# An mLSTM cell with a quick-GELU layer: order of the second chunk's loads, issuer of the first chunk's stores, order of the first gelus

## The chip, the cores and the metric

The kernel runs on one core of a Trainium2 chip. The metric is the device time of one execution in microseconds (us). A core has five engines that run side by side, each through its own list of instructions in order: PE (matmul), DVE (vector), ACT (scalar, with activation functions), POOL, and SP, which here only issues DMA transfers. They meet at semaphores.

## The reference

The first part is an mLSTM cell over 4 batches, 8 heads, 768 time steps and a head size of 40. The second is a feed-forward layer with the quick GELU.

```python
for t in range(S):
    m_new = np.maximum(f_gate[:, :, t] + m, i_gate[:, :, t])
    f_stab = np.exp(f_gate[:, :, t] + m - m_new)
    i_stab = np.exp(i_gate[:, :, t] - m_new)
    m = m_new
    C = f_stab * C + i_stab * einsum('bhd,bhe->bhde', v_t, k_t)
    n = f_stab * n + i_stab * k_t
    h_tilde = einsum('bhde,bhe->bhd', C, q_t)
    denom = np.maximum(np.abs(sum(n * q_t)), 1.0)
    y[:, :, t] = sigmoid(o_gate[:, :, t]) * h_tilde / denom
x = y.transpose(0, 2, 1, 3).reshape(B * S, H * D)      # 3072 x 320
h = x @ w_in                                            # 320 x 2048
out = (h * sigmoid(1.702 * h)) @ w_out                  # 2048 x 320
```

## The kernel before, in words

Time is cut into six chunks of 128 steps (`w` from 0 to 5). For each chunk the mLSTM is worked out as attention within the chunk plus a state carried from the chunks before; then the 512 rows of the chunk (4 batches of 128) go through the feed-forward layer. While the layer of chunk `w` runs on PE, the attention of chunk `w + 1` is put between its matmuls, in steps that `attention` lists.

No scheduler moves instructions. Each engine runs its instructions as the Python calls stand, so an instruction that waits holds back all behind it on its engine. Every DMA is given one of eight completion semaphores; before it is used again, its next user waits until the DMA that had it has landed. At most eight transfers are therefore under way from SP.

The parts that the change and the prediction touch:

- Loads. `load` brings a chunk's k, v or output gates (`eo`, 640 KB in one DMA; `eo` has one buffer). `load_blocks` brings k and q a second time in small blocks (`k_bl`, `q_bl`, 16 DMAs each) that DVE then transposes to `kT` and `qT` (L302). `spread` brings the rows of running maxima (`m_row`) to all partitions as `wt` (L317, 4 DMAs).
- Weights. 20 pieces come in by `fetch` (L166), 0 to 9 of `w_in` and 10 to 19 of `w_out`. They land in `big`, `bits` or `xs`, and `convert` turns each into its rounded form, with two instructions on ACT (L228, L229) and four on DVE (L232 to L237). Pieces 16 to 19 use rooms that pieces 10 to 12, or others, had before. The table `beside` says when pieces are converted and when later ones are fetched; pieces 16 and 17 hold rows of `w_out` that the third group of four of `down` (n = 2) reads.
- Chunk 0. The first two hidden blocks are multiplied before the main loop (`full_rows`, L714 and L737), and their gelus (L765) stand at the head of the loop. The others go through `up` (L458, L464, gelus L468). `down` (L561) then makes 16 blocks, four for each batch; the last of a batch copies the sum from PSUM (L565, DVE, into one of two `o_sb` buffers) and stores it (L566).
- Attention of chunk 1 beside those blocks: `columns`; `weights` (exponentials L335, POOL's mask L337; for batch 0 also the tanh of the gates, L340); `scores` (PE L348, DVE L350); `values` (PE L360 and L365, DVE L380 to L390); `seam` (transposes L399, and ACT's copy to `xT`, L400); `new_states` (L425) and `carry` (L433).
- Chunks 1 to 5. `up_fast` and `down_fast` take seven products of half-size blocks in place of eight. `up_fast` first makes sums of `xT` (L501 to L504), six products L513, then the remaining rows L541; sums on DVE are L521, gelus on ACT L525. In its first call `next_keys` stands between (sums of weights L489, the next chunk's `gates`, and transposes L302). The sums of `w_out` are L580.

SP's list in the stretch of interest is: pieces 10 to 15; the gates `eo` of chunk 1; 16 `k_bl`; 4 `wt`; pieces 16 and 17; 16 `q_bl`; v; pieces 18 and 19; k; the gates i and f of chunk 2; 16 `k_bl` and 16 `q_bl` of chunk 2; the four stores of chunk 0; then chunk 2's `m_row`.

Of the kernel before, what the change touches and what calls it, by code (L numbers as in the profile page):

```python
# [22 lines left out]
L = 128  # L23
# [11 lines left out]
def kernel(  # L35
# [12 lines left out]
    nc = tc.nc  # L48
    B, H, S, D = q.shape
# [44 lines left out]
    def load_gates(w):  # L94
        for dst, src in ((f_sb, f_gate), (i_sb, i_gate)):
            dst[w] = ld.tile([BH, L], FP, tag="fi", bufs=4, name="fi")
            nc.sync.dma_start(out=dst[w], in_=src[:, :, w * L:(w + 1) * L].rearrange("b h s -> (b h) s"))

    def load(w, what, bs=slice(0, B)):
        hs = slice(bs.start * H, bs.stop * H)  # L100
        for c in what:
            if c == "o" and w not in eo:
                eo[w] = ld.tile([L, BH, D], FP, tag="eo", bufs=1, name="eo")
            dst, src = {"k": (k_st, k), "q": (q_st, q), "v": (v_st, v), "o": (eo.get(w), o_gate)}[c]
            nc.sync.dma_start(out=dst[:, hs, 0:D],
                              in_=src[bs, :, w * L:(w + 1) * L, :].rearrange("b h s d -> s (b h) d"))

    def load_blocks(w, which=slice(0, 2)):
        both = (k_bl, k), (q_bl, q)
        for dst, src in both[which] if isinstance(which, slice) else both[which:which + 1]:  # L110
            for two in range(2):
                for d in range(0, D, 32):
                    n = min(32, D - d)
                    r = two * 64 + d
                    for g in range(L // 32):
                        t = w * L + g * 32
                        nc.sync.dma_start(
                            out=dst[r:r + 32, :, g, 0:n],
                            in_=src[:, two:H:2, t:t + 32, d:d + n].rearrange("b j s d -> s (b j) d"))
# [36 lines left out]
    def fetch(n):  # L156
        if 6 <= n < 10:
            bits[n] = gp.tile([128, 512, 2], U32, tag="g", name="bits")
        else:
            room = xs if n == 19 else big[:, n if n < 6 else (n - 10) % 6, :]  # L160
            bits[n] = room.bitcast(U32).rearrange("p (a two) -> p a two", two=2)
        for r, c, src in pieces[n][1]:
            dst = bits[n][r, c].rearrange("p a two -> p (a two)")
            if len(src.shape) == 3:
                dst = dst.rearrange("p (j m) -> p j m", j=src.shape[1])
            nc.sync.dma_start(out=dst, in_=src)  # L166
# [131 lines left out]
    def transposes(w, b):  # L298
        for bl, st, dst, name in ((k_bl, k_st, kT, "kT"), (q_bl, q_st, qT, "qT")):
            dst[w, b] = work.tile([128, NP, L], FP, tag=name, bufs=4, name=name)  # L300
            if w:
                V.transpose(out=dst[w, b].rearrange("p j t -> p (j t)"),  # L302
                            in_=bl[:, b * NP:(b + 1) * NP].rearrange("p j g c -> p (j g c)"))
                continue
            pt = ps_a.tile([128, NP, L], FP, tag="a", name="p_t")
            for p in range(NP):
                h = b * H + 2 * p
                T.transpose(pt[:, p, :], st[:, h:h + 2, :].rearrange("p a b -> p (a b)"), ident)
            if b == 0:
                keep_busy(1)  # L310
            A.copy(out=dst[w, b], in_=pt)

    def spread(w):

        for b in range(B):
            x = wt[w, b] = work.tile([L, NP, 2, L], FP, tag="wt", bufs=4, name="wt")
            nc.sync.dma_start(out=x.rearrange("s p i t -> s (p i) t"),  # L317
                              in_=m_row[w][b * H:(b + 1) * H, :].unsqueeze(0).to_broadcast([L, H, L]))
# [237 lines left out]
    def down(w, b, n):  # L556
        if n == 0:
            o_ps[w, b] = (ps_m if b < 2 else ps_x).tile([128, DM], FP, tag="mx"[b // 2], name="p_out")
        po = o_ps[w, b]
        for f in range(n * 4, n * 4 + 4):  # L560
            T.matmul(po, gs[w, f // 2][:, f % 2, b * L:(b + 1) * L], w_out_sb[:, f, :], start=(f == 0),  # L561
                     stop=(f == NF - 1))
        if n == NF // 4 - 1:
            o = op.tile([128, DM], FP, tag="o", name="o_sb")
            V.tensor_copy(out=o, in_=po)  # L565
            nc.sync.dma_start(out=out[b * S + w * L:b * S + (w + 1) * L, :], in_=o)  # L566

# [8 lines left out]
    def weight_sums(n):  # L578
        out_, in0, in1 = ((t1, w01, w00), (t2, w11, t1), (t4, w10, t2), (w01, w11, w01))[n]
        V.tensor_tensor(out=out_, in0=in0, in1=in1, op=OP.subtract)  # L580
# [153 lines left out]
    for j in range(2):  # L734
        for i in range(2):
# [2 lines left out]

    beside = {0: ((5,), range(10, 16)), 1: ((6, 7, 8), ()), 2: ((9, 10, 11), (16, 17)), 3: ((12, 13, 14), (18, 19)),
              4: ((15,), ()), 5: ((16,), ()), 10: ((17,), ()), 12: ((18,), ()), 14: ((19,), ())}

    def weights_in(n):
        done, ahead = beside.get(n, ((), ()))
        for p in done:
            convert(p)
        for p in ahead:
            fetch(p)
# [8 lines left out]
    for w in range(NW):  # L758
        more = w + 1 < NW
        for j in range(NF // 2):  # L760
            if w == 0 and j == 0:
                weights_in(0)
                for pair_ in range(2):
                    for i, g in enumerate(hidden_of(0, pair_)):
                        A.activation(out=g, in_=first[pair_][i], func=AF.Gelu_apprx_sigmoid)  # L765
            elif w == 0 and j % 2 == 0:
                weights_in(j // 2)
                up(j, j == 2)
            elif w and j % 4 == 0:
                up_fast(w, j, next_keys if more and j == 0 else None)  # L770
            if j == 0 and more:
                load(w + 1, "o")
            if w == 0 and j == 0:
                load_blocks(1, 0)
                spread(1)
            if w == 1 and j == 3:
                weight_sums(3)
            if more:
                if j == 4:
                    if w == 0:  # L780
                        load_blocks(1, 1)
                    load(w + 1, "v")
                    if w:
                        spread(w + 1)
                if j == (4 if w else 6):
                    load(w + 1, "k")
                if w and j == 3:
                    for b in range(2, 4):
                        transposes(w + 1, b)
            if w and j in (3, 7):  # L790
                hidden_sums(w, 0, (j // 4 * 2, j // 4 * 2 + 1), 1, 2)
                if j == 3:
                    hidden_sums(w, 0, (0, 1), 3, 4)
        side = attention(w + 1) if more else []
        if w == 0:

            blocks = [(lambda b=b, n=n: down(w, b, n)) for ns in ((0, 1), (2,), (3,)) for b in range(B) for n in ns]
            stops = (0, 1, 5, 7, 9, 11, 13, 15)
        else:
            blocks = down_fast(w, 0) + down_fast(w, 1)  # L800
            stops = (0, 1, 2, 4, 8, 10, 11, 12)
        for i, block in enumerate(blocks):
            if w == 0:
                weights_in(4 + i)
                if i == 0:
                    load_gates(2)
                if i == 2:
                    first_sums((0, 1))
                if i == 10:
                    load_blocks(2)  # L810
                for b in {2: (0, 1), 7: (2,), 9: (3,)}.get(i, ()):
                    transposes(1, b)
            elif w + 2 < NW and i == 0:
                load_gates(w + 2)
                load_blocks(w + 2)
            block()
            if i in stops and side:
                run(side.pop(0))
            if w == 1 and i == 1:
                weight_sums(2)  # L820
            if w:
                for at, c, *what in ((0, 0, (2, 3), 3), (1, 0, (2, 3), 4), (1, 1, range(4), 1),
                                     (5, 1, range(2), 2), (6, 1, range(2, 4), 2), (7, 1, range(4), 4)):
                    if i == at:
                        hidden_sums(w, c, *what)
                if i == 2 and not more:
                    hidden_sums(w, 1, range(4), 3)
            elif i in (12, 14):
                weight_sums(i // 2 - 6)
# [30 lines left out]
```

## Time and profile before

| | us |
|---|---|
| median of 9 runs | 490.92 |
| lowest and highest | 489.18, 495.72 |
| the profiled execution | 489.18 |
| its span | 487.5 |
| PE busy in it | 481.4 (99%) |
| DVE busy | 343.0 (70%) |
| ACT busy | 220.9 (45%) |
| POOL busy | 61.2 (13%) |

The profile is of one execution, the fastest of the nine. Its span runs from the first to the last instruction; 1.7 us of its time lie outside. A line of a timeline gives the start, the length, the engine, the line of the kernel, the operation, what it writes and reads, and in brackets the idle time before it and what ended that. Lines marked SPq are DMA issues, whose length is that of the issue; the transfer itself lands later. The chunks begin on PE's feed-forward products at about 24 us (chunk 0), 115 (chunk 1), 194, 270, 346 and 422.

### The profile page before, as it was taken

What the parts mean: (1) busy time and instruction counts of PE and PEld (TensorE: products, weight loads), DVE (VectorE), ACT (ScalarE), POOL (GpSimd) and SP (SyncE); (2) the same over time, 40 slices, a digit from 0 to 9 for tenths busy, and PEclk for the clock granted to TensorE, in tenths of its full rate; (3) what the DMA queues carried; (4) which work ended last, traced back from release to release, by engine and by line L of the source; (5) the groups of instructions that cost most, each with busy time, mean ns of one, the idle gap of its engine ahead of it and who ended that gap; (6) DMA issues with size and microseconds to landing.
All of it is one profiled execution on the core that took longest, in us unless ns stands there. A gap on an engine that the chain in (4) does not pass through costs nothing. (4 is left out here: it accounts for less than half of the span.)

```text
span 487.5 us, 10441 instructions
## 1 busy us (share of the span) xinstructions
PE 481.4 (99%) x4076; PEld 396.7 (81%) x4076; DVE 343.0 (70%) x855; ACT 220.9 (45%) x575; POOL 61.2 (13%) x103
## 2 busy tenths in 40 slices
PE   8999999999999999999999999999999999999997
PEld 5874456777678999787999877999977999977997
DVE  8789768887978965667776586686576786254831
ACT  6766767302458501476700465900364920255300
POOL 4030002231000340000332000232000120000000
PEclk9999999999999999999999999999999999999999
DMA  9999799563996200996100796300393000000000
GB/s 135 182 290 338 98 267 171 71 73 77 133 227 63 29 28 15 158 215 75 15 29 1 117 253 75 32 28 3 72 261 31 1 7 24 28 2 0 1 27 28
DMA packets 175953, 44.87 MB, mean 92 GB/s; under 512 B 164352, under 2 KB 169504, under 8 KB 175904
## 3 DMA queue, kind: packets, MB, share of 16 engines
q1 hardware_dynamic: 175904, 44.21, 48.4%
q8 instruction: 32, 0.52, 0.4%
q14 instruction: 17, 0.14, 0.1%
HBM read 40.17 MB, written 4.01 MB: 91 GB/s over the span
## 5 line engine op out<-in xcount | busy, mean ns | idle before, releaser
L610 PE MATMUL p_out<-w_out_sb,g 128*128 128x160 f32 x480 | 69.8, 301 | 0.0
L400 ACT COPY xT<-p_x 128x384 f32<-128x384 f32 x24 | 11.0, 480 | 128.0 <-PE p_x L399 128.0
L610 PEld LDWEIGHTS p_out<-w_out_sb,g 128*128 128x128 f32 x480 | 66.4, 190 | 0.9
L521 DVE TENSOR_TENSOR g<-p_u,g 128x256 f32<-128x256 f32 x80 | 33.6, 424 | 44.7 <-PE p_u L513 35.1
L518 ACT COPY g<-p_u 128x256 f32<-128x256 f32 x120 | 43.0, 376 | 43.4 <-PE p_u L513 39.2
L525 ACT ACTIVATE g<-g 128x256 f32<-128x256 f32 x120 | 42.3, 423 | 40.2 <-DVE g L521 40.2
L337 POOL TENSOR_SCALAR_AFFINE_SELECT wt<-wt 128x1024 f32<-128x1024 f32 x20 | 22.7, 1134 | 232.5 <-ACT wt L335 201.8
L615 DVE TENSOR_TENSOR o_sb<-o_sb,p_out 128x160 f32<-128x160 f32 x70 | 21.3, 316 | 42.3 <-PE p_out L610 41.9
L335 ACT ACTIVATE wt<-wt,cols 128x128 f32<-128x128 f32 x160 | 48.0, 394 | 0.0
L513 PE MATMUL p_u<-xT,w_in_sb 128*128 128x256 f32 x160 | 39.2, 383 | 0.0
L513 PE MATMUL p_u<-xs,big 128*128 128x256 f32 x160 | 37.9, 380 | 0.2 <-issue 0.2
L541 PE MATMUL p_v<-xT,w_in_x 64*128 64x512 f32 x80 | 37.2, 603 | 0.0
L541 PE MATMUL p_u<-xT,w_in_x 64*128 64x512 f32 x80 | 37.0, 602 | 0.0
L561 PE MATMUL p_out<-w_out_sb,g 128*128 128x320 f32 x128 | 36.2, 437 | 0.0
L350 DVE TENSOR_TENSOR wt<-p_s,wt 128x512 f32<-128x512 f32 x48 | 30.4, 682 | 7.7 <-POOL wt L337 5.5
L610 PE MATMUL p_out<-t,big 128*128 128x160 f32 x240 | 35.5, 301 | 0.0
L513 PEld LDWEIGHTS p_u<-xT,w_in_sb 128*128 128x128 f32 x160 | 29.6, 190 | 5.7 <-DVE o_sb L615 1.5
L513 PEld LDWEIGHTS p_u<-xs,big 128*128 128x128 f32 x160 | 29.9, 190 | 5.1 <-issue 0.6
L610 PEld LDWEIGHTS p_out<-t,big 128*128 128x128 f32 x240 | 33.3, 190 | 0.2
L561 PEld LDWEIGHTS p_out<-w_out_sb,g 128*128 128x128 f32 x128 | 23.8, 190 | 10.1 <-issue 0.5
L521 DVE TENSOR_TENSOR g<-p_v,g 128x256 f32<-128x256 f32 x80 | 29.8, 413 | 0.0
L541 PEld LDWEIGHTS p_v<-xT,w_in_x 64*128 64x128 f32 x80 | 14.1, 186 | 16.0 <-issue 16.0
(168 smaller groups left out, 863.4 us busy)
## 6 DMA issues: line engine op xcount, KB each, us to landing
wt<-m_row SPq DMA_DIRECT2D x20, 512.0 KB, 6.9
out_dram<-o_sb SPq DMA_DIRECT2D x24, 160.0 KB, 1.8
eo<-in_o_gate_dram SPq DMA_DIRECT2D x5, 640.0 KB, 5.5
v_st<-in_v_dram SPq DMA_DIRECT2D x5, 640.0 KB, 8.8
k_st<-in_k_dram SPq DMA_DIRECT2D x5, 640.0 KB, 11.4
big<-in_moe_w_in_dram SPq DMA_DIRECT2D x5, 512.0 KB, 6.0
k_bl<-in_k_dram SPq DMA_DIRECT2D x40, 64.0 KB, 2.6
q_bl<-in_q_dram SPq DMA_DIRECT2D x40, 64.0 KB, 2.6
```

The source lines that it names most:

```text
L335: A.activation(out=x[:, h, :], in_=x[:, h, :], func=AF.Exp, scale=-1.0, bias=cols[w][:, b * H + h:b * H + h + 1])
L337: G.affine_select(out=x, in_=x, compare_op=OP.is_ge, fill=0.0, base=0, pattern=[[0, H], [1, L]], channel_multiplier=-1)
L350: V.tensor_tensor(out=wt[w, b][:, :, i, :], in0=pw[i], in1=wt[w, b][:, :, i, :], op=OP.mult)
L400: A.copy(out=xT[w][:, :, b, :], in_=px)
L513: T.matmul(p[k][:, ts[t]], a[:, k // 2, k % 2 * 128:(k % 2 + 1) * 128], b, start=first, stop=True, skip_group_check=True)
L518: A.copy(out=g[k][i][:, ts[t]], in_=chain[k][:, ts[0]])
L521: V.tensor_tensor(out=g[k][i][:, ts[t]], in0=p[k][:, ts[pt]], in1=g[k][i][:, ts[t]], op=OP.add)
L525: A.activation(out=dst, in_=dst if src is None else src, func=AF.Gelu_apprx_sigmoid)
L541: T.matmul(p[k], w_in_x[r, k, :], x[r, 2, :], start=False, stop=True, skip_group_check=True)
L561: T.matmul(po, gs[w, f // 2][:, f % 2, b * L:(b + 1) * L], w_out_sb[:, f, :], start=(f == 0), stop=(f == NF - 1))
L610: T.matmul(po, a(f), b[:, f, :], start=(f == 0), stop=(f == NH - 1))
L615: V.tensor_tensor(out=dst, in0=x, in1=po, op=OP.add)
```

## The change

Four edits, and none in what PE runs or in which order it runs it:

1. `down` issues its four stores (chunk 0 alone uses `down`) from ACT's list in place of SP's.
2. The second chunk's `q_bl` loads follow its `k_bl` and `wt` loads at once. Before, `eo` stood ahead of the `k_bl`, and pieces 16 and 17 ahead of the `q_bl`. SP's list becomes: pieces 10 to 15; 16 `k_bl`; 4 `wt`; 16 `q_bl`; piece 16; `eo`; piece 17; v; and on as before.
3. Piece 16 is converted ahead of block 4 of `down` in place of block 1, so on ACT it follows the exponentials and the tanh of batch 0 (L335, L340), and on DVE it follows the transposes and the first sums of weights. The transposes of chunk 1 stand ahead of those sums (`first_sums`).
4. At the head of the loop the gelus of the first hidden block, with the load of their table, stand ahead of the conversion of piece 5.

```diff
@@ -563,7 +563,7 @@
         if n == NF // 4 - 1:
             o = op.tile([128, DM], FP, tag="o", name="o_sb")
             V.tensor_copy(out=o, in_=po)
-            nc.sync.dma_start(out=out[b * S + w * L:b * S + (w + 1) * L, :], in_=o)
+            nc.scalar.dma_start(out=out[b * S + w * L:b * S + (w + 1) * L, :], in_=o)
...
-    beside = {0: ((5,), range(10, 16)), 1: ((6, 7, 8), ()), 2: ((9, 10, 11), (16, 17)), 3: ((12, 13, 14), (18, 19)),
-              4: ((15,), ()), 5: ((16,), ()), 10: ((17,), ()), 12: ((18,), ()), 14: ((19,), ())}
+    beside = {0: ((5,), range(10, 16)), 1: ((6, 7, 8), ()), 2: ((9, 10, 11), (16,)), 3: ((12, 13, 14), (18, 19)),
+              4: ((15,), ()), 8: ((16,), ()), 10: ((17,), ()), 12: ((18,), ()), 14: ((19,), ())}
...
             if w == 0 and j == 0:
-                weights_in(0)
                 for pair_ in range(2):
                     for i, g in enumerate(hidden_of(0, pair_)):
                         A.activation(out=g, in_=first[pair_][i], func=AF.Gelu_apprx_sigmoid)
+                    if pair_ == 0:
+                        weights_in(0)
...
-            if j == 0 and more:
-                load(w + 1, "o")
             if w == 0 and j == 0:
                 load_blocks(1, 0)
                 spread(1)
+                load_blocks(1, 1)
             if w == 1 and j == 3:
                 weight_sums(3)
             if more:
+                if j == (0 if w else 4):
+                    load(w + 1, "o")
                 if j == 4:
                     if w == 0:
-                        load_blocks(1, 1)
+                        fetch(17)
                     load(w + 1, "v")
                     if w:
                         spread(w + 1)
...
                 weights_in(4 + i)
                 if i == 0:
                     load_gates(2)
+                for b in {2: (0, 1), 7: (2,), 9: (3,)}.get(i, ()):
+                    transposes(1, b)
                 if i == 2:
                     first_sums((0, 1))
                 if i == 10:
                     load_blocks(2)
-                for b in {2: (0, 1), 7: (2,), 9: (3,)}.get(i, ()):
-                    transposes(1, b)
```

## The prediction

> **What bounds the kernel now.** I read the page's engine rows first, then the table of windows for the same stretch of each chunk, then the timelines of PE, DVE, ACT and SP around the places that the change touches. The page:
>
> ```profile
> PE 481.4 (99%) x4076; PEld 396.7 (81%) x4076; DVE 343.0 (70%) x855; ACT 220.9 (45%) x575; POOL 61.2 (13%) x103
> PEclk9999999999999999999999999999999999999999
> ```
>
> PE looks full, at an unthrottled clock, so only lost PE time can be won. But matmul ends are modelled, and a busy PE can hide waits. The first half of the hidden layer is the same list of matmuls in chunks 1 and 2 (six products, then the rest rows of L541), so its length compares them:
>
> ```profile
> 115.39:131.74 16.35, 16.08 (x69) 10.45 (x65) 15.53 (x34) 6.58 (x15) 0.15 (x1) 1.00 0.60 94
> 193.67:208.01 14.34, 14.34 (x67) 10.32 (x65) 10.31 (x27) 6.58 (x15) 0.00 (x0) 1.00 0.92 155
> ```
>
> Columns: window, length, then busy time of PE, PEld, DVE, ACT, POOL. Chunk 1 takes 16.35 us for what chunk 2 does in 14.34: 2.01 us lost, and DVE is busy 15.53 of the 16.35 us. The PE timeline shows where:
>
> ```profile
> 115.39 2.28 PE L513 MATMUL p_u<-xT,w_in_sb 128*128 128x256 f32 x8
> 117.51 2.18 PE L513 MATMUL p_v<-xT,w_in_sb 128*128 128x256 f32 x8
> 119.89 1.97 PE L513 MATMUL p_u<-xs,big 128*128 128x256 f32 x8 [0.20 <-issue]
> ...
> 127.03 1.12 PE L541 MATMUL p_v<-xT,w_in_x 64*128 64x512 f32 x2
> 128.11 0.69 PE L541 MATMUL p_u<-xT,w_in_x 64*128 64x512 f32 x1
> ```
>
> Undisturbed products follow each other every 1.72 us; here the steps are 2.12 and 2.38, and the third starts just after DVE made its operand. L541 needs 4.71 us to 131.74 against 3.64 in chunk 2 (204.37 to 208.01): p_u waits for the sums that DVE makes late. DVE is late for this reason:
>
> ```profile
> 114.63 0.49 DVE L565 COPY o_sb<-p_out 128x320 f32<-128x320 f32 x1 [2.75 <-DMA out_dram<-o_sb]
> 115.04 1.48 DVE L580 TENSOR_TENSOR t<-w_out_sb,t 128x1280 f32<-128x1280 f32 x1
> 116.44 0.48 DVE L565 COPY o_sb<-p_out 128x320 f32<-128x320 f32 x1
> 116.84 2.04 DVE L433 TENSOR_TENSOR state<-p_c,state 40x328 f32<-40x328 f32 x4
> 118.90 0.43 DVE L501 TENSOR_TENSOR xs<-xT 128x256 f32<-128x256 f32 x1
> 119.36 0.42 DVE L502 TENSOR_TENSOR xs<-xT,xs 128x256 f32<-128x256 f32 x1
> ```
>
> The copy of batch 2's output waits 2.75 us for one of two o_sb buffers, held by batch 0's store. That store was ready at 105.9 (its L565 began at 105.42), but stood on SP behind 32 block loads of chunk 2:
>
> ```profile
> 94.25 8.85 SPq L117 DMA_DIRECT2D k_bl<-in_k_dram  x16
> 103.19 9.19 SPq L117 DMA_DIRECT2D q_bl<-in_q_dram  x16
> 112.48 4.80 SPq L566 DMA_DIRECT2D out_dram<-o_sb  x4
> ```
>
> A store lands a median 1.8 us after issue. From 118.90 to L521 at 127.63 DVE has no pause, so its lateness is passed on to both PE losses. One more place has no slack:
>
> ```profile
> 78.45 0.71 DVE L302 STREAM_TRANSPOSE qT<-q_bl 128x512 f32<-128x512 f32 x1 [1.48 <-DMA q_bl<-in_q_dram]
> ```
>
> Chunk 1's qT is ready at 79.16 and PE's scores start at 79.21. Here PE lost nothing, but a later transfer costs PE its whole delay.
>
> **The change part by part.** PE's order of instructions is unchanged, so every gain or cost is a wait.
>
> Stores on ACT. Four issues of 0.33 to 0.43 us (L566) leave SP and go to ACT. Store 0 can go at 105.9 and lands at about 108; store 1 (copy done 107.8) at about 110. Batch 2's copy is then free once DVE ends its values work (L390 at 111.38 + 0.49 = 111.9): 2.7 us earlier. L580 (1.5) runs to 113.9; batch 3's copy waits for PE's last block (to 113.7) and ends 114.4. L433 needs p_c (PE 114.03 to 115.4): two of its four can start at 114.75, the end is 116.8 against 118.9. So L501 and L502 come 2.1 us earlier: operand at 117.7, while the third product, at chunk 2's pace (193.67 to 197.37, 3.70), wants it at 119.1. L521 would start at 125.5; chunk 2's pace puts L541 at 115.39 + 10.70 = 126.1. Both losses go: 2.0 us.
>
> What waits behind the stores. ACT's xT copies (L400) of batches 2 and 3: the first moves from 107.65 to about 108.4, the second from 114.14 to about 114.9, ending 115.4. DVE reads xT at 116.8, and p_x is needed back by the second product's tiles at about 117.5: cost 0. Its price begins when an ACT issue takes over 2 us instead of 0.4. On SP, the built program's waits put the stores on completion semaphores 6, 2, 7 and 1 of eight, which SP's block loads reuse: chunk 2's 3rd, 5th, 10th and 12th q_bl load now wait for the four stores. The last store lands at about 114.8 + 1.8 = 116.6, four more issues follow at 0.53 spacing, and landing takes 2.2 to 2.6: about 121.2. DVE's qT for chunk 2 comes at 125.74 - 2.1 = 123.6. Hidden, slack 2.4.
>
> Here a rule speaks against the change. The Trainium skill, DMA: Bandwidth & Descriptors, section Issuing engines are not separate DMA queues: DMAs from several engines run on the same 16 engines and interleave, so another issuer saves only sequencer issue time, usually small relative to the DMA. By that this part is worth about 0, the sum 490.9. The row has the opposite proportion: 18.2 us of SP issue (94.25 to 112.4) ahead of a 1.8 us store. I take the row: -2.0.
>
> Loads in another order. Sixteen q_bl loads go ahead of the gates (eo, 640 KB), piece 16 (three loads) and piece 17 (two). All these DMAs still precede v. q_bl, landed at 78.4 before, is no longer behind eo and the pieces. Eo alone took 4.1 us (previous load landed at 43.04 + 5.0 = 48.0, eo at 43.61 + 8.5 = 52.1), the five loads 61.19 to about 71.1 overlapped with wt, some 3 us. So q_bl lands by about 72, six us early. The profiled execution gains 0 to 0.1 (PE waited at most that).
>
> The price is eo: before landed at 52.1; now before piece 17 and v. V landed at 76.67 + 5.9 = 82.6; less v's 4.1 and piece 17's 1.9 leaves 76.6 at latest; with SP less held up, 74. ACT's tanh (L340, at 73.49 before) waits for it, and behind it stand piece 16's conversion and two rows of exponentials. Landing X, then tanh 1.28, first half of a conversion 0.67, DVE's four instructions 2.44 (70.74 to 73.18), L350 twice 1.25: wt for PE's values at X + 5.6. PE wants it at 84.81, so PE waits X - 79.2, and not at all at 76.6. DVE, 1.3 us late after that, has a pause of 1.25 before L380 at 86.58 to catch up. Piece 17 is converted by about 85.5; its first use is PE's third group after 87.56. Cost 0, both bounds -0.1 and +1.
>
> First gelus ahead of conversion 5. ACT's two gelus of the first pair and the table load (1.28) come before two instructions of 0.67. Its conversion starts at about 37.1 instead of 33.92; DVE wanted it at 37.31 and gets it at 37.8: 0.5 us late, and at 49.19 it paused 0.44 anyway. PE ran through L737 into L458 at 37.36 without a pause. 0, gain at most 0.1.
>
> Sum for the profiled execution (span 487.5, 489.18 with 1.7 around it): -2.0, so 487.2. It is the fastest of nine; the median, 490.92, is 1.74 above it. Against the median: 488.9. Of the 1.74, some should be late transfers that the two slackless places (qT at 79.16, the store behind SP's loads) hand to PE, and that now have 2 us or more of cover. Between 0 and 1.74, I take 0.7, an estimate, since the rest can arise in the first 30 us, which do not change. Forecast 488.2.
>
> **The rivals.** All of the scatter is late q_bl: 487.2. For: zero slack. Against: ACT and PE also wait for loads in the first 30 us. None of it is: 488.9, within 0.5%.
>
> The gain is half given back: the stores' issue on ACT takes 2 to 3 us when SP's loads fill the queue (SP's own k_bl issue at 44.03 belongs to a run of 16 taking 14.72 us), so xT is late and the chunk keeps about 1.5 us of loss: 490.4.
>
> Slower: eo lands late and stops ACT at L340. It decides from X = 79.2, cancels the gain at 81.2, and makes it slower by over 0.5% (2.45 us) from 83.7. At 85, which needs eo to land after where v does now, PE loses 5.8: 490.92 + 3.8 = 494.7. For: ACT is in order and eo is now among the last loads of a stretch with DMA shares of 0.9. Against: the sum of transfers before v is unchanged.
>
> **How the numbers follow.** 0.45 for 488.2 (487.4 to 489.0; about 0.40 of it under 488.47), 0.15 for 487.2, 0.20 for 488.9, 0.12 for 490.4, 0.08 for slower. What one can tell from no change is about 0.5%, here 2.45 us. Faster by more: 0.40 + 0.15 = 0.55; same 0.05 + 0.20 + 0.12 = 0.37; slower 0.08. The range 486.4 to 490.6 leaves out the slower case and the outer ends of 490.4 and 487.2.
>
> **What would show it.** Right: L565's second copy near 111.9 with no wait for a DMA, L501 near 116.8, the stretch from the first p_u to the second half's last product as long as chunk 2's 14.3, scores still at 79.2 with qT ready before 75. Wrong: a long wait of ACT at L340 that shows as a PE pause before 84.81 or at 87 to 100, L400 after 117, or qT of chunk 2 waiting for q_bl after 124.

## The result, and the profile after

| | before | after |
|---|---|---|
| median | 490.23 (55 runs) | 487.30 (18 runs) |
| lowest and highest | 488.85, 495.72 | 486.81, 489.15 |
| the profiled execution | 489.18 | 487.75 |
| its span | 487.5 | 486.0 |

After over before is 0.9938, with a 95% interval of 0.9922 to 0.9955: 0.6% faster, and the interval lies wholly below 1. The medians lie 2.93 us apart, the two profiled executions only 1.43, since that of before was a fast one (1.05 below its median) and that of after was not (0.45 above). So a comparison of the two traces shows half of the gain. Seen over all runs, the lowest times are 2.04 apart (488.85 and 486.81), and the median stands 1.38 above the lowest before, 0.49 above it after. (The median of before is now 490.23 over 55 runs; the 490.92 that the prediction started from was that of nine of them.)

The page's engine row, and the row of windows for the first half of chunk 1's hidden layer:

```profile
PE 479.4 (99%) x4076; PEld 397.3 (82%) x4076; DVE 342.3 (70%) x855; ACT 220.8 (45%) x575; POOL 61.7 (13%) x103
115.81:130.29 14.48, 14.48 (x68) 11.55 (x64) 13.66 (x32) 6.58 (x15) 0.15 (x1) 1.00 0.77 107
```

The stretch takes 14.48 us where it took 16.35: 1.87 less, and close to chunk 2's 14.34. It starts 0.42 later than before (115.81 against 115.39). -1.87 and +0.42 make -1.45, about the difference of the profiled pair. (0.34 of the 0.42 is there already at 37.7 us, 0.10 is won at 79 us and 0.19 lost at 100 us, as shown below.) The PE timeline in it:

```profile
115.81 1.99 PE L513 MATMUL p_u<-xT,w_in_sb 128*128 128x256 f32 x8
117.64 1.89 PE L513 MATMUL p_v<-xT,w_in_sb 128*128 128x256 f32 x8
119.37 1.89 PE L513 MATMUL p_u<-xs,big 128*128 128x256 f32 x8
```

The steps between the products are 1.83 and 1.73 us, in place of 2.12 and 2.38. DVE shows why:

```profile
112.22 0.48 DVE L565 COPY o_sb<-p_out 128x320 f32<-128x320 f32 x1
115.39 2.04 DVE L433 TENSOR_TENSOR state<-p_c,state 40x328 f32<-40x328 f32 x4 [0.66 <-POOL state L412]
117.46 0.42 DVE L501 TENSOR_TENSOR xs<-xT 128x256 f32<-128x256 f32 x1
```

The copy of batch 2's output no longer waits for a DMA, and the first sum for the third product is made at 117.46 in place of 118.90, ahead of the product that wants it at 119.37. The other side of the edit is ACT's timeline (ACTq are its DMA issues):

```profile
107.81 2.24 ACTq L566 DMA_DIRECT2D out_dram<-o_sb  x2
110.09 0.48 ACT L400 COPY xT<-p_x 128x384 f32<-128x384 f32 x1 [9.31 <-PE p_i L365]
112.73 2.40 ACTq L566 DMA_DIRECT2D out_dram<-o_sb  x2
115.17 0.48 ACT L400 COPY xT<-p_x 128x384 f32<-128x384 f32 x1 [4.60 <-DMA out_dram<-o_sb]
```

One issue takes 0.34 to 0.38 us; the groups are longer because the second issue waits for its copy. The last copy of `xT` ends at 115.65 (115.17 + 0.48), DVE reads it at 117.46.

The other place of interest is 73 to 101 us, where chunk 1's queries, gates and v come in (timelines of DVE, ACT and PE):

```profile
73.52 0.71 DVE L302 STREAM_TRANSPOSE qT<-q_bl 128x512 f32<-128x512 f32 x1 [2.95 <-DMA big<-in_moe_w_out_dram]
79.29 1.27 ACT L340 ACTIVATE eo<-eo 128x1280 f32<-128x1280 f32 x1 [6.48 <-DMA eo<-in_o_gate_dram]
83.63 1.29 DVE L350 TENSOR_TENSOR wt<-p_s,wt 128x512 f32<-128x512 f32 x2
79.45 1.16 PE L348 MATMUL p_s<-qT,kT 40*128 40x128 f32 x16
85.05 1.13 PE L360 MATMUL p_o<-v_st,wt 128*64 128x41 f32 x32
100.20 1.32 PE L360 MATMUL p_o<-v_st,wt 128*64 128x41 f32 x32
```

The last query load landed at 73.34 (issued at 71.10, 2.2 us on the way), and they are transposed at 73.52, five us ahead of PE's scores at 79.45; before, they were ready 0.05 ahead of them. (The bracket names a load of `big`; what ended a wait is inferred.) The 40 matmuls in front of the scores started at 68.51, 10.94 us ahead of them, in place of 11.04 before: this is the 0.10. But ACT now stands 6.48 us for the gates, which land at 79.27. The product made from them (L350) ends at 84.92, and PE's values start at 85.05. The slack that the queries gained has gone to the gates: 0.13 us is left there. v is close behind: it landed at 84.49 (issued at 78.01), 0.56 us before PE wanted it. DVE runs about 2 us late from 84 on, and PE loses 0.19 of it at 100.20 (1.32 where such a group takes 1.13).

### The profile page after: what moved, and what is told of

Same layout as the page of the kernel before. It is cut to its first block, busy times and chain, and to the rows that moved or that the text cites. A ratio compares the mean times of both kernels' runs of the same rounds, so it can differ in the third digit from the quotient of the medians.

```text
span 486.0 us, 10444 instructions
## 1 busy us (share of the span) xinstructions
PE 479.4 (99%) x4076; PEld 397.3 (82%) x4076; DVE 342.3 (70%) x855; ACT 220.8 (45%) x575; POOL 61.7 (13%) x103
## 5 line engine op out<-in xcount | busy, mean ns | idle before, releaser
L335 ACT ACTIVATE wt<-wt,cols 128x128 f32<-128x128 f32 x160 | 48.0, 392 | 0.0
L561 PE MATMUL p_out<-w_out_sb,g 128*128 128x320 f32 x128 | 36.2, 437 | 0.0
L350 DVE TENSOR_TENSOR wt<-p_s,wt 128x512 f32<-128x512 f32 x48 | 30.4, 681 | 7.9 <-POOL wt L337 5.5
L561 PEld LDWEIGHTS p_out<-w_out_sb,g 128*128 128x128 f32 x128 | 23.8, 190 | 10.1 <-issue 0.5
```

The source lines that it names most:

```text
L335: A.activation(out=x[:, h, :], in_=x[:, h, :], func=AF.Exp, scale=-1.0, bias=cols[w][:, b * H + h:b * H + h + 1])
L350: V.tensor_tensor(out=wt[w, b][:, :, i, :], in0=pw[i], in1=wt[w, b][:, :, i, :], op=OP.mult)
```

## The experiments

The question after the result was what each edit gives, and what made the executions scatter less. The theory to be tested: the stores give about 2 us in every execution, by a buffer that is held behind SP's list; the order of loads gives the rest, in executions in which transfers land late; the gelus give nothing. The rivals: all of it is the stores; or the issuer matters and not the buffer; or the first gelus, where executions also differ, carry the scatter. Each ratio is against runs of before on the same chip, whose medians went from 490.87 to 492.4, so only ratios are compared.

**The stores alone** (before with edit 1):

```diff
-            nc.sync.dma_start(out=out[b * S + w * L:b * S + (w + 1) * L, :], in_=o)
+            nc.scalar.dma_start(out=out[b * S + w * L:b * S + (w + 1) * L, :], in_=o)
```

> The kernel before with one edit, the four stores of chunk 0 issued by ACT. Known so far: the whole change takes the median from 490.2 to 487.3 us (2.9), while the two profiled spans differ by 1.5, and the stretch of chunk 1 (first p_u to the end of L541) shrank from 16.35 to 14.48 us. Theory A (two causes: the stores free DVE, worth 1.9 in every execution, and the load order takes away late queries, worth about 1 in the median): 488.3, ratio 0.996, the stretch about 14.4, and the wide upper tail of the runs (to 495 us) stays. Theory B (the stores are the whole of it, since jitter of SP's 32 block loads reaches PE through them alone): 487.3, ratio 0.994, tail gone. Theory C (what matters is the load order): 490, the stretch still over 16.

Measured: 489.11 (16 runs, 487.81 to 493.35), ratio 0.9949 [0.9927, 0.9972]. The row of windows for the stretch:

```profile
116.51:131.00 14.49, 14.49 (x69) 11.50 (x65) 13.68 (x32) 6.59 (x15) 0.16 (x1) 1.00 0.80 108
```

Nearly the whole of the stretch's loss goes with this line (chunk 2 takes 14.34). Five of the 16 runs are still above 490.

**The order of loads alone** (edits 2 and 3; stores on SP, gelus as before; only the loads are shown):

```diff
-            if j == 0 and more:
-                load(w + 1, "o")
...
                 load_blocks(1, 0)
                 spread(1)
+                load_blocks(1, 1)
...
+                if j == (0 if w else 4):
+                    load(w + 1, "o")
                 if j == 4:
                     if w == 0:
-                        load_blocks(1, 1)
+                        fetch(17)
```

> The kernel before with the load order alone (queries of chunk 1 ahead of its gates and of pieces 16 and 17, piece 16 converted later, transposes ahead of the first sums); stores stay on SP, gelus as before. Theory A: the stretch of chunk 1 stays at about 16.3 us and DVE still waits some 2.7 us at the copy of batch 2; the median falls by about 1 us to 489.2 (ratio 0.998) and the runs are closer together, because qT is no longer on the edge. Theory B: no change of the median (0 to 0.5 us slower, as the gates now hold up ACT), tail still there. Theory C: 487.3.

Measured: 491.49 (14 runs) where before had 491.30 on this chip, ratio 0.9979 [0.9954, 1.0004]. A gain is not shown; nor is one of about 1 us (0.998) excluded. Row of windows, then DVE and PE:

```profile
115.25:132.36 17.11, 16.08 (x68) 10.45 (x65) 16.30 (x35) 6.59 (x15) 0.16 (x1) 1.00 0.55 89
115.25 0.49 DVE L565 COPY o_sb<-p_out 128x320 f32<-128x320 f32 x1 [3.51 <-DMA out_dram<-o_sb]
117.60 0.70 PE L513 MATMUL p_u<-xT,w_in_sb 128*128 128x256 f32 x2 [0.78 <-DVE o_sb L565]
```

In this execution the stretch became longer, 17.11 us. SP's list runs 0.7 us later (chunk 2's `k_bl` from 94.94 in place of 94.25), so the stores at its end are issued from 113.08 in place of 112.48, the held buffer comes free later (a wait of 3.51 in place of 2.75), and PE now stops for 0.78 us. So the two edits do not simply add up in the traces: here the order of loads costs 0.76 us in the stretch while the stores stand behind it.

**The gelus alone** (edit 4):

```diff
             if w == 0 and j == 0:
-                weights_in(0)
                 for pair_ in range(2):
                     for i, g in enumerate(hidden_of(0, pair_)):
                         A.activation(out=g, in_=first[pair_][i], func=AF.Gelu_apprx_sigmoid)
+                    if pair_ == 0:
+                        weights_in(0)
```

> The kernel before with the first two gelus, and their table load, ahead of the conversion of piece 5, and nothing else. Theories A, B and C: 0 within 0.1%; PE runs through L737 into L458 without a pause in both. If the gelus mattered in executions that were not profiled, the median would fall by 0.3 us or more.

Measured: 491.16 (22 runs, up to 495.79), ratio 1.0017 [0.9993, 1.0040]; the stretch takes 16.23. A gain is not shown, and the runs are no narrower.

**Two more buffers for the outputs, stores left on SP.** Batches 2 and 3 copy into a part of `big` that is not in use:

```diff
-            o = op.tile([128, DM], FP, tag="o", name="o_sb")
+            o = op.tile([128, DM], FP, tag="o", name="o_sb") if b < 2 else big[:, b - 2, 0:DM]
```

> The kernel before with one edit: outputs of batches 2 and 3 of chunk 0 are copied to two idle parts of another buffer in place of the two o_sb buffers, so DVE's copy need not wait for a store; the stores stay on SP behind the 32 block loads. If the store matters only through the buffer that it holds (theories A and B), this gives the same as stores on ACT: the copy of batch 2 near 112, the stretch about 14.4, 488.3 by A and 487.3 by B. If instead the place in SP's list matters in another way (the stores in SP's way of m_row or of chunk 2's loads), it gives nothing.

Measured: 488.50 (8 runs), ratio 0.9925 [0.9894, 0.9956]. Row of windows, DVE, and SP's issues:

```profile
118.02:132.60 14.58, 14.58 (x68) 10.94 (x64) 13.67 (x32) 6.58 (x15) 0.15 (x1) 1.00 0.51 80
114.43 0.48 DVE L565 COPY big<-p_out 128x320 f32<-128x320 f32 x1
115.41 0.91 SPq L566 DMA_DIRECT2D out_dram<-o_sb  x2
```

The stores leave SP at 115.41, even later than before, and the stretch still takes 14.58. So what cost the time was the buffer that waited for the late store. The same profile is of a late execution (490.05 in a kernel whose lowest is 487.30), and PE's list of waits shows the place that had no slack:

```profile
PE p_s L348 <- DVE qT L302: 1.2, 1, 1.2
PE p_h L458 <- ACT g L765: 0.7, 1, 0.7
```

The last `q_bl` landed at 81.05, and PE's scores waited 1.2 us. The second row is the wait that the gelu edit would take away. It is there, 0.7 us, in such an execution; a PE that runs that much earlier reaches the queries that much earlier, which would explain why the gelus alone gain nothing, but that link was not tested by itself.

**The stores alone, again** (the one line of the first experiment), to see a late execution of the old order:

> Stores on ACT and nothing else, a second time, to stand beside the runs of this group. Theory A2: median 1.2 to 1.8 us above that of the two other orders of loads (488.6 to 489), ratio 0.995 to 0.996, with a quarter of the runs over 490. If the load order is worth nothing, its median equals that of the kernel with gates and v sooner within 0.3 us.

Measured: 488.98 (22 runs, 487.45 to 494.38), ratio 0.9960 [0.9940, 0.9980]; seven runs above 490. The profiled execution is the slowest of them. DVE and PE:

```profile
82.19 0.71 DVE L302 STREAM_TRANSPOSE qT<-q_bl 128x512 f32<-128x512 f32 x1 [1.87 <-DMA q_bl<-in_q_dram]
82.96 1.98 PE L348 MATMUL p_s<-qT,kT 40*128 40x128 f32 x16 [3.53 <-DVE qT L302]
84.87 7.06 PE L561 MATMUL p_out<-w_out_sb,g 128*128 128x320 f32 x16
91.86 1.13 PE L360 MATMUL p_o<-v_st,wt 128*64 128x41 f32 x32
```

The queries landed at 82.17, 3.7 us later than in the profile of before, and PE stood 3.53. Then the 16 matmuls of L561 take 7.06 us, where the same group took 4.57 before. The rows of windows say why (the number after POOL's is the granted clock):

```profile
83.00:86.00 3.00, 3.00 (x18) 2.48 (x19) 2.05 (x4) 0.90 (x4) 0.00 (x0) 0.52 1.42 193
88.00:90.00 2.00, 2.00 (x5) 1.22 (x5) 1.90 (x3) 1.23 (x2) 0.00 (x0) 0.52 0.99 262
90.00:92.00 2.00, 2.00 (x13) 1.17 (x12) 0.00 (x0) 0.00 (x0) 0.00 (x0) 1.00 1.47 171
```

After the pause PE ran at half its clock until about 90 us. From the scores to the values it took 8.90 us (82.96 to 91.86) against 5.60 in after (79.45 to 85.05). So one late set of loads cost 3.53 by the pause and 3.30 by the clock, 6.8 us. The kernel before loads in the same order, and several of its runs at 493 to 496 have a mean clock of 0.993 to 0.997 too (h2's profiled one has 0.993); no trace of them exists.

**The change without the gelus, and the change once more**, side by side. The first undoes edit 4 in after:

```diff
+                weights_in(0)
                 for pair_ in range(2):
...
-                    if pair_ == 0:
-                        weights_in(0)
```

> Stores on ACT and the new load order, without the gelu edit (the gelus and their table load after the conversion of piece 5, as before). Measured so far: stores alone 0.9949 with a tail to 493.4, loads alone 0.9979, gelus alone 1.0017, the whole change 0.9938 with no run over 489.2. Theory A2: the load order gives its gain only once the stores are off SP (alone it puts SP's list some 2 us later and so the stores too), and it removes the late queries; then this kernel equals the whole change, 0.993 to 0.994, with few runs over 490. Theory D: the gelu edit is what removes the tail (in one profile PE waited 0.7 us at L458 for the gelus of L765); then this stays at 0.995 with the tail of the stores alone.

> The changed kernel once more, so that it stands on the same chip and beside the same runs of before as the others of this group. All theories: 0.993 to 0.994, runs within about 2 us of each other.

Measured: without the gelus 488.00 (8 runs), ratio 0.9923 [0.9896, 0.9949]; the change 487.74 (15 runs, 486.98 to 493.56), ratio 0.9952 [0.9927, 0.9977]. The intervals overlap, so no difference is shown. (The 2 us by which the first expectation has SP's list late are those of after, whose chunk 2 `k_bl` start at 96.25; in e2 it was 0.7.) Both profiled executions are late ones, and show where the slack is gone. First f1's PE, then f2's ACT, DVE and PE:

```profile
87.03 1.14 PE L360 MATMUL p_o<-v_st,wt 128*64 128x41 f32 x32 [2.27 <-DMA v_st<-in_v_dram]
81.86 1.27 ACT L340 ACTIVATE eo<-eo 128x1280 f32<-128x1280 f32 x1 [8.95 <-DMA eo<-in_o_gate_dram]
86.20 1.29 DVE L350 TENSOR_TENSOR wt<-p_s,wt 128x512 f32<-128x512 f32 x2
87.53 1.14 PE L360 MATMUL p_o<-v_st,wt 128*64 128x41 f32 x32 [2.31 <-DVE wt L350]
```

In f1 the gates landed at 81.15, the product was ready at 86.80, and v landed at 86.89, which came last. In f2 the gates landed at 81.84, and the product was ready at 87.49, as the prediction's price has it (landing + 5.6 is 87.44). The bracket puts PE's wait down to it, but PE can begin with the first of the two instructions of L350, as it does in h0 below, and that one ended at 86.89; v landed at 87.39 (issued at 80.76, 6.6 us on the way), and PE followed 0.14 us later, in f1 0.13. By these times v ended both pauses, and the gates alone would have made f2's some 0.5 us shorter (an estimate: first product against v). Pauses of 2.27 and 2.31 left the granted clock at 1.00.

**The gates later still**, behind v, to measure the slower rival:

```diff
-                if j == (0 if w else 4):
+                if w and j == 0:
                     load(w + 1, "o")
...
                     load(w + 1, "v")
+                    if w == 0:
+                        load(1, "o")
```

> The changed kernel with the gates eo of chunk 1 issued behind v: one DMA moved by two places, to try the price of the slower rival on purpose. Price by the prediction: L350's product ready at eo's landing + 5.6. In the whole change v landed at 84.5 and eo took some 4 us, so eo lands about 84.5 and the product is ready at 90.1: PE waits some 5 us at the values of batch 0 (L360) and the median is about 492.3, ratio 1.004 against before, slower than the change by 1%. Rival (ACT's lateness is taken up by pauses of DVE and PE, so that the place of eo costs less): under 2 us.

Measured: 496.84 (4 runs), ratio 1.0107 [1.0063, 1.0150]: slower than before. The profiled execution took 495.71, its span 494.0. ACT and PE:

```profile
85.42 1.27 ACT L340 ACTIVATE eo<-eo 128x1280 f32<-128x1280 f32 x1 [11.41 <-DMA eo<-in_o_gate_dram]
90.49 0.44 PE L360 MATMUL p_o<-v_st,wt 128*64 128x41 f32 x4 [4.18 <-DVE wt L350]
86.00:90.40 4.40, 0.31 (x2) 0.00 (x0) 2.89 (x6) 4.40 (x12) 0.20 (x1) 0.84 1.07 226
92.00:95.00 3.00, 3.00 (x44) 2.82 (x43) 2.83 (x6) 2.72 (x8) 0.00 (x0) 0.50 0.42 45
95.00:98.00 3.00, 3.00 (x18) 2.29 (x17) 2.83 (x9) 0.00 (x0) 0.69 (x2) 0.87 0.00 0
```

The gates landed at 85.40, the first of the two instructions of L350 ended at 90.44, and PE began at 90.49. Its pause of 4.18 (and 0.25 for the second product) is close to the 5 that was expected. But the clock was 0.50 again behind it (the last three lines are rows of windows). From the first scores to batch 1's values PE took 20.10 us (80.64 to 100.74) against 13.18 in after (79.45 to 92.63): 6.92 more, 4.43 by pauses and 2.49 by the clock. The expectation had only the first.

**The gates sooner.** Two ways to give them slack: behind the queries but ahead of piece 16, and first of all, as before, with only the queries ahead of pieces 16 and 17.

```diff
-                if j == (0 if w else 4):
+                if j == 0:
                     load(w + 1, "o")
```

and, for the second:

```diff
+            if j == 0 and more:
+                load(w + 1, "o")
             if w == 0 and j == 0:
                 load_blocks(1, 0)
...
-                if j == (0 if w else 4):
-                    load(w + 1, "o")
```

> The changed kernel with the gates eo of chunk 1 issued right after the queries, ahead of piece 16 and not behind it. In the profile of the whole change eo landed at 79.3, and L350's product was ready at 84.9 for PE's 85.05: no slack left. By the price in the prediction (product ready at landing + 5.6) eo at about 77.7 gives product at about 83.5, and PE's 0.19 us pause at the values of batch 2 (100.2) goes. Theory A2: 0.1 to 0.5 us faster than the whole change in the median, ratio 0.993. If the gates aren't near the edge: no difference.

> The changed kernel with the gates eo of chunk 1 ahead of all its block loads, as in the kernel before; queries still ahead of pieces 16 and 17. Queries should land some 4 us later than in the whole change (about 77) and still 2 us before PE needs qT; eo lands near 53, ACT no longer stops at L340, DVE is 2 us earlier from 84 to 109. Theory A2 (slack decides, wherever it is missing): 0 to 0.5 us faster than the whole change. If only early queries remove the tail: slower than the whole change by 0.5 to 1 us, with runs over 490.

Measured: 487.39 (10 runs), ratio 0.9925 [0.9899, 0.9951], and 488.36 (7 runs), ratio 0.9938 [0.9913, 0.9962]. In the first the gates land at 76.91, L350 ends at 83.78 (it starts at 82.49), and the 0.19 us at 100 are gone. The next transfer is then the last one to come, PE at its values:

```profile
84.94 1.14 PE L360 MATMUL p_o<-v_st,wt 128*64 128x41 f32 x32 [0.16 <-DMA v_st<-in_v_dram]
```

In the second, piece 16 comes late instead: ACT waited 4.59 for it, and L350 ends at 84.76 (it starts at 83.47), where PE's values start at 84.56; with the first of its two products made, they need not wait.

**The gates and v sooner**: the first of these two, with v ahead of piece 17.

```diff
                 if j == 4:
+                    load(w + 1, "v")
                     if w == 0:
                         fetch(17)
-                    load(w + 1, "v")
```

> The changed kernel with the gates eo ahead of piece 16 and v ahead of piece 17. In the profile with eo ahead of piece 16 PE waited 0.16 us for v at 84.94, so v was the next on the edge; with v two places on it should land near 83 and piece 17, now near 85, is still ready for its first use near 89. If the runs' spread comes from transfers that land late by 1 to 3 us in some executions (theory A2), the median is that of the best so far, 487.2 to 487.4 (ratio 0.9925), and the upper runs come down, nearly all under 489. If spread arises elsewhere (the first 30 us), the upper runs stay.

Measured: 487.83 (7 runs, 487.14 to 490.21), ratio 0.9941 [0.9913, 0.9969]. A gain over g1 is not shown. In its profiled execution piece 17 was the late one (ACT waited 1.45 for it), and v landed at 84.34 and not at the 83 expected.

**Slack everywhere.** The tanh of the gates is needed only at L388, but stood on ACT ahead of the exponentials that PE's values wait for. This version takes it behind the conversion of piece 17, which lets the gates be loaded last (after the queries, piece 16, v and piece 17). Against after:

```diff
-        if b == 0:
+        if b == 0 and w > 1:
...
-                if j == (0 if w else 4):
+                if w and j == 0:
                     load(w + 1, "o")
                 if j == 4:
+                    load(w + 1, "v")
                     if w == 0:
                         fetch(17)
-                    load(w + 1, "v")
+                        load(1, "o")
...
+                if i == 7:
+                    A.activation(out=eo[1], in_=eo[1], func=AF.Tanh, scale=0.5)
```

> The changed kernel with v right behind piece 16, then piece 17, then the gates eo of chunk 1, and the tanh of those gates on ACT behind the conversion of piece 17, ahead of the exponentials of batch 2, in place of behind those of batch 0. Nothing but DVE's L388 (at 88.2) now waits for eo. Estimates from the traces: v lands near 80 (PE wants it at 85), piece 17 near 81.5 (wanted by 87), eo near 85 (tanh done 86.5, wanted at 88.2, and DVE has over 1 us to lose after that); ACT no longer stops at L340 and DVE is not 2 us late from 84 to 109. Theory A2: no PE pause from 79 to 115 in the profile, median 486.9 to 487.3, ratio about 0.992, and no run over 489.5. If the spread of the runs comes from the first 30 us, which are unchanged, runs over 489.5 stay and the median equals that of the change.

Measured: 487.21 (6 runs, 487.07 to 487.71), ratio 0.9909 [0.9880, 0.9938]. ACT, DVE and PE:

```profile
84.52 1.27 ACT L815 ACTIVATE eo<-eo 128x1280 f32<-128x1280 f32 x1 [2.37 <-DMA eo<-in_o_gate_dram]
81.03 1.29 DVE L350 TENSOR_TENSOR wt<-p_s,wt 128x512 f32<-128x512 f32 x2
84.73 1.13 PE L360 MATMUL p_o<-v_st,wt 128*64 128x41 f32 x32
99.88 1.13 PE L360 MATMUL p_o<-v_st,wt 128*64 128x41 f32 x32
```

The gates land at 84.49, as late as in h0, and nothing waits: the product is ready at 82.32, v landed at 79.5, and PE has no pause from 79 to 115. Its median is the lowest of all and its runs spread over 0.64 us, though of six runs only. Its ratio is the lowest too, against the slowest runs of before (11, median 492.40); its interval and that of after overlap, so a gain over after is not shown.

## Why the prediction was right, and where it was not

The forecast was 488.2; 487.30 came. Taken apart, by its own terms:

| term | predicted | measured |
|---|---|---|
| the base, median of before | 490.92 | 490.23 |
| stores, every execution | -2.0 | -2.04 (lowest times), -1.87 (the stretch in the trace) |
| scatter | -0.7 | -0.89 (median above lowest, 1.38 to 0.49) |
| sum | 488.2 | 487.30 |

The last two terms make up the measured difference by the way they are taken, so the table gives sizes and not causes; those are in the experiments. The base is most of the miss: nine runs gave a median 0.7 us above that of 55. As a ratio the forecast was 488.2 / 490.92 = 0.9945, and 0.9938 was measured. That 487.30 lies next to the 487.2 of the first rival (all of the scatter is late queries) is luck of the base: with 490.23 that rival gives 486.9 (-2.0 and -1.38) and the forecast 487.5.

- **Stores.** The step held in its parts. L565 came at 112.22 (predicted 111.9), L501 at 117.46 (116.8, with a chunk that itself starts 0.42 later), the last copy of `xT` ended at 115.65 (115.4). The couplings through completion semaphores were there too: SP's third `q_bl` load of chunk 2 stood until 111.20 for the first store's, the last one landed at 121.66 (predicted 121.2), and the queries' transposes came at 124.30. Hidden, by the 2.6 us that the prediction put at 2.4.
- **The rule weighed there.** The Trainium skill, DMA: Bandwidth & Descriptors, section Issuing engines are not separate DMA queues, says that another issuer saves only sequencer issue time. That stands: e4 gets the same stretch without another issuer. What the row had, and the sentence's "usually small" does not cover, is 18.2 us of issue ahead of one store. The row decided rightly.
- **Order of loads, its gain.** Expected were 0 to 0.1 in the profile, where 0.10 came, and a part of the scatter, on the ground that the queries had no slack. That place is shown (e4's 1.2 us, h2's 3.53). Of the runs with the stores alone 12 of 38 were above 490 (e1 and h2), of those with the new order as well 3 of 41 (the 18 runs of after, f1, f2), though not on the same chips. Chip by chip one can count the runs with a mean clock of 0.997 or less, which in h2 and h0 was the mark of a long pause: with the old order 21 of 93 (before, e1, e3, e4), with the new one 1 of 14 (e2); on the next 7 of 27 (before) and 3 of 40 (f1, f2, g1, g2); on the third 12 of 50 (before, h2) and 0 of 7 (h1); on the last 3 of 11 (before) and 0 of 6 (i1). (g1, g2, h1 and i1 have variants of the new order.) The medians' ratios overlap (0.9949 and 0.9960 against 0.9938, 0.9923 and 0.9952), so its size in the median, some 0.8 us by the means of these ratios, is an estimate. That without the first edit it lengthens the stretch (e2) was not foreseen: the prediction costed the parts one by one.
- **Order of loads, its price.** Here a term was mis-sized. The gates were to land at 74, at 76.6 at latest, and landed at 79.27. The bound of 76.6 took v's landing as it was before, 82.6, and subtracted from it; but v landed at 84.49, 1.9 us later (SP stood 2.9 us at piece 17, so v was issued 1.34 later, and it took 6.5 us in place of 5.9), and the gates came 5.2 ahead of v and not 6.0. As for the 74, the queries took until 73.3 rather than 72, and the gates were issued only at 73.11 and landed 6.2 us after that, beside other transfers. The formula behind it held (X + 5.6 gives 84.87; L350 ended at 84.92), so the change ran on the very edge of the slower rival, which was put at 79.2. In the late executions f1 and f2 it was v that crossed the edge, for pauses of 2.27 and 2.31; the prediction had taken v's landing as unchanged. The pause of 1.25 in which DVE was to catch up was too small for this: DVE came to L350 3.15 us late (83.63 against 80.48) and stayed 2 us late until 109, for a PE loss of 0.19, a small form of the prediction's own sign of being wrong.
- **The slower rival's price.** The product was ready 5.6 us after the landing in f1, f2 and h0 too (in h0 85.40 and 91.03). The pause is X - 79.2 less what PE itself is late, 4.8 for h0, and 4.43 came, in two parts, since the first matmuls need only the first of the two products. f2 does not test it, since v came last there. But for long pauses this is not the whole price: in h0's trace the clock took 2.49 us more. By the prediction's sum X = 85.4 gives about 495; the traced execution took 495.71 and the median of the four was 496.84.
- **Half given back.** ACT's issues took 0.34 to 0.38 us, not 2 to 3; that rival did not occur.
- **Gelus.** Costed at 0, and 0 lies within the interval (e3); f1 and f2 do not differ clearly.

What stays open is why executions differ, but the traces narrow it: the late transfers are not slower, they are issued later. SP's issues of chunk 1's blocks, two lines of before, then two of h2:

```profile
44.03 14.72 SPq L117 DMA_DIRECT2D k_bl<-in_k_dram  x16
65.50 11.06 SPq L117 DMA_DIRECT2D q_bl<-in_q_dram  x16
47.09 15.06 SPq L117 DMA_DIRECT2D k_bl<-in_k_dram  x16
69.44 10.97 SPq L117 DMA_DIRECT2D q_bl<-in_q_dram  x16
```

In h2 the queries are issued 3.9 us later, and the last two loads land 2.2 to 2.6 us after their issue, as in before (2.5 to 2.6). The gates took 6.2 us from issue to landing in after and 6.3 in f2, but were issued at 73.11 and at 75.57. Of h2's 3.9 us, 3.1 are there when the `k_bl` begin, in a part of SP's list that the orders of loads and stores tried here leave as it is. PE too is late there in some executions: its first L458 starts at 38.58 in e1, 38.86 in e4 and 38.89 in h0, against 37.36 in before, and no edit here reaches that but the gelus (0.7 of e4's). This is the part of the scatter that the prediction left to the first 30 us. What holds SP back there was not tested; the versions differ only in what is waiting when it happens.

## What to carry to other kernels

Where a copy waits for an output buffer, look at what the store stands behind in its issuer's list, not at how long the store takes: another issuer or another buffer each took 1.8 to 1.9 us off the stretch here, while a better order of loads in the same list made the wait longer in the execution that was traced. Give every transfer that the matmuls need a slack of the size by which executions differ (here up to 3.7 us), and move work that nothing urgent needs, such as this tanh, out of the line in front of it, rather than passing the last place from one transfer to the next. Read the lowest time and the median apart: what an edit does to every execution shows in the first and in a trace, what it does to late ones only in the distance between them.

## What was unexpected of the hardware

A pause of PE has a second price from some length on. Pauses of 2.27 and 2.31 us left the granted clock at 1.00; with those of 3.53 (h2) and 4.18 (h0) it fell to 0.50. The rows of windows give the times. In h2 a mean of 0.52 over 83 to 86 us leaves 0.12 us at 1.00, so the clock fell at 83.1; by the same sum over 88 to 90, 0.08 us at 1.00, it came back at 89.9. In h0 a mean of 0.84 over 86.0 to 90.4 means 1.4 us at 0.50, so it fell at 89.0, 1.5 us before PE's pause ended; 0.87 over 95 to 98 puts the return at 95.8. Both times the half clock lasted 6.8 us, and what it cost is nearly half of the part in which PE worked: 6.8 us of it in h2 (3.30 lost), 5.3 in h0 (2.49 lost).

The Trainium skill, TensorE: Matmul & The Clock Gate, Part 1: The HAM clock gate, puts the fall to half rate after an idle window of about 3.4 us, and the return after about 3.4 us of sustained work. The lengths of the four pauses lie on the sides of 3.4 that fit this, but the clock fell 3.7 us after PE's last matmul in h2 and only about 2.7 us after it in h0, and the return came after 7 us (h2) and 5.3 us (h0) of work, so these traces bear out neither figure closely. By the mean clocks the half clock does not always last as long: 6.8 us of it make the mean of 0.993 that both traced executions have, while 0.996 and 0.997, which most of the other such runs have, make 2.5 to 4.4 us (an estimate from the rounded means).
